# First stage of a Fourier layer: input tiles in spread pairs, batch one kept in SBUF and written by quads

## The chip, the cores and the metric

One core of one Trainium2 chip runs the whole program; the host only lays out inputs before and the output after. The metric is the device time of one execution in microseconds; several executions are timed and their median counts.

## The reference

Two batches of 3008 rows of 256 numbers go through a Fourier layer (transform along the sequence, a complex matrix per frequency, a soft threshold, the inverse transform), and the 6016 resulting rows through two feed-forward layers.

```python
X = np.fft.rfft(x, axis=1)                       # x: (2, 3008, 256)
Yr = Xr @ w_r - Xi @ w_i + b_r
Yi = Xr @ w_i + Xi @ w_r + b_i
Y  = shrink(Yr, 0.01) + 1j * shrink(Yi, 0.01)    # sign(a) * max(|a| - 0.01, 0)
y  = np.fft.irfft(Y, n=3008, axis=1)
h  = y @ w_in                                    # 256 -> 2048
y  = (h * clip(h + 3, 0, 6) / 6) @ w_out
y  = (silu(y @ w_gate) * (y @ w_val)) @ w_out2   # 256 -> 1536 -> 256
```

## The kernel before

The engines are TensorE (PE, with its weight loads PEld), VectorE (DVE), ScalarE (ACT), GpSimd (POOL) and SyncE (SP). The order of instructions is written out by hand: a list `seq` of steps that a loop runs one after the other, each appending to every engine's own queue. An engine takes its queue strictly in order and waits on semaphores. SP issues nearly all DMAs and ACT those that store what ACT and DVE evicted; an issue waits for the data that it needs, for room in the tile that it fills, and for an earlier DMA whose semaphore it shares (eight semaphores go round among the DMAs of SP and ACT). SP's and ACT's transfers each have a ring on the same 16 DMA engines.

The transform of length 3008 = 47 x 64 is split. **Stage one** (`pre`, lines 239 to 254) takes, for each batch, eight tiles of 94 rows (padded to 96) by 4 x 256 columns; a tile is two matmuls of 512 columns with the table `fwd1`, evicted by ACT (first half) and DVE (second half) to a ring tile `bs`, and written to a scratch in memory `Bd` by ACT. `load_x` reads x three tiles ahead, into two pairs of buffers. **Stage two** (`s2`, lines 281 to 294) works on a quad, four of the 24 frequency groups at a time, six quads (Q) per batch: `load_q` (lines 273 to 279) reads a table `m` and the quad's 16 of the 96 rows of `Bd`, over all columns, as `z`. So z of any quad needs all eight tiles of its batch in memory. ACT and DVE evict the result as a high and a low part, X. **The product** (`ln`, lines 305 to 326) multiplies with the complex weights `linh` and `linl`, two halves per quad with 24 matmuls each, reads a table `n`, and steps a conversion `conv1`. **The last step** (`ia`, lines 328 to 336) goes back within the quad and writes `Cd`.

`conv1` (class `Convert`, lines 137 to 189) turns the first feed-forward weights, which arrive as 64-bit words in 32 pieces `st` of 256 KB, into a high and a low part `w1h` and `w1l`: one piece per step, in stages on DVE and ACT. `Convert.load` on SP waits for a free `st` buffer of four.

`seq` (lines 366 to 378) runs stage one of batch one and three tiles of batch two, then stage two of quad 0, and then for each quad p: half a product, half a last step of quad p - 1, a tile of batch two while there are any, stage two of quad p + 1 (which issues the reads of quad p + 2), the other half of the product, another tile, another half of a last step. From quad 8 on, `unit()` mixes in the first feed-forward layer, in blocks of about 500 tokens; `load_ct` and `post` read `Cd` and finish the inverse transform of a block. The second feed-forward layer follows.

`prepare` (lines 228 to 237) issues the reads of the weights `lin`, of the bias and of the table `inv2` on POOL's queue and splits lin into `linh` and `linl` there. Ahead of everything PE runs three warm-up matmuls on zeros.

Of the kernel before, what the change touches and what calls it, by code (L numbers as in the profile page):

```python
# [40 lines left out]
def dft_tables():  # L41


    tp = 2 * np.pi
    n1 = np.arange(N1)
    f = np.zeros((N1, NG, 2))
    for g in range(NG):
        a = tp * ((n1 * g) % N1) / N1
        f[:, g, 0], f[:, g, 1] = np.cos(a), -np.sin(a) * (g > 0)
    fwd1 = np.zeros((2, N1, NG, 2, 2))  # L50
    for q in range(2):
        fwd1[q, :, :, q, :] = f
# [20 lines left out]
    out = {"fwd1": fwd1, "inv2": fwd1.T, "fwd2": fwd2, "inv1": inv1}  # L73
    return {n: np.ascontiguousarray(v, dtype=np.float32) for n, v in out.items()}
# [3 lines left out]
def fourier_moe_kernel(ctx: ExitStack, tc: tile.TileContext, x, lin, bias, w1, w2, fwd1, inv2, fwd2,  # L78
# [9 lines left out]
    Bd = [dram.tile([GW, NJ * DIM], F32, name=f"Bd{b}") for b in range(NB)]  # L88
# [32 lines left out]
    fwd1_sb = misc.tile([QP, GW], F32, name="fwd1_sb")  # L121
# [15 lines left out]
    class Convert:  # L137
# [11 lines left out]
        def load(self, i):  # L149
            t = wst.tile([128, 256], I64, tag="st", name="st", bufs=4)  # L150
            nc.sync.dma_start(t, self.pieces[i][0])
# [24 lines left out]
        def high(self, i):  # L176
            nc.scalar.copy(self.pieces[i][1], self.full[i])

        def low(self, i):
            _, hi, lo = self.pieces[i]  # L180
# [10 lines left out]
    def pieces(p, name, src, nf, n, into):  # L191
        out = []
        for f in range(nf):
            t = [p.tile([128, n, 256], F32R, name=f"{name}{i}_{f}") for i in "hl"]
            into[f] = t
            out += [(src[:, f, j], t[0][:, j], t[1][:, j]) for j in range(n)]
        return Convert(out)
# [7 lines left out]

    def ring4(name):
        return ap_.tile([128, 4 * DIM], F32, tag="bc", name=name, bufs=4)


    NT = NJ // 4  # L210
    xt = {}
# [8 lines left out]
    for n in range(3):  # L220
        load_x(n)
# [4 lines left out]
    conv1 = pieces(w1p, "w1", w1, KF1, 2, W1)  # L226

    def prepare():
# [3 lines left out]
        nc.gpsimd.dma_start(inv2_sb, inv2)  # L232
# [5 lines left out]

    def pre(n):
        b, i = divmod(n, NT)  # L240
        load_x(n + 3)
        bs = ring4(f"bs{b}_{i}")
        for h in range(2):
            p = psf[0]([GW, 512], f"p1_{b}_{i}_{h}")
            nc.tensor.matmul(p, fwd1_sb, xt[n][:QP, h * 512 : (h + 1) * 512], start=True, stop=True)
            o = bs[:GW, h * 512 : (h + 1) * 512]
            if h == 0:
                nc.scalar.copy(o, p)
            else:
                nc.vector.tensor_copy(o, p)  # L250
# [22 lines left out]
    def load_q(b, Q):  # L273
        if (b, Q) in z_t or Q >= NQ:
            return
        if Q not in m_t:
            m_t[Q] = table("m", fwd2, Q, f"m{Q}", 6)
        z_t[b, Q] = ap_.tile([128, 4, DIM], F32, tag="z", name=f"z{b}_{Q}", bufs=3)
        nc.sync.dma_start(z_t[b, Q], bview[b][:, Q * 4 : Q * 4 + 4, :])

    def s2(b, Q, dh):

        if dh == 0:
            X[b, Q] = [ap_.tile([128, 2, 4, 3 * K2], F32R, tag=f"x{k}", name=f"x{k}_{b}_{Q}", bufs=2) for k in "hl"]
# [75 lines left out]
    def pre_conv(n):  # L360
        pre(n)
        if n > NT:
# [3 lines left out]
    seq = P[:1] + [prepare] + P[1:NT] + [lambda: load_q(0, 0)] + P[NT : NT + 3] + S(0)  # L366
    rest = P[NT + 3 :]
    for p in range(len(ORDER)):
        l, a = L(p), A(p - 1)
        some, rest = rest[:2], rest[2:]  # L370
        u = [lambda: unit()] if p >= FROM else []
        seq += [l[0], a[0]] + u + some[:1] + S(p + 1)[:1] + u + S(p + 1)[1:] + [l[1]] + u + some[1:] + [a[1]] + u
        if p == NQ:
            seq += [lambda: load_ct(blocks[0])]
# [23 lines left out]
    def pair(p, tag):  # L398
        return [p.tile([128, 2, BLK], F32R, tag=f"{tag}{i}", name=f"{tag}{i}", bufs=2) for i in "hl"]
# [164 lines left out]
    conv2 = Convert2([(w2[:, f, j], None, None) for f in range(KF2) for j in range(3)])  # L564
# [244 lines left out]
```

## Time and profile before

| | us |
|---|---|
| median of 3 runs | 1247.07 |
| range of the runs | 1246.85 to 1248.23 |
| the profiled execution, its time | 1247.67 |
| the profiled execution, its span in the trace | 1245.9 |
| idle time of PE between 28.0 and 34.3 us | 6.3 |

The median is the metric. The profile is of one execution whose own time, 1247.67, is 1.77 above its span, as the time counts what lies around the first and the last instruction. In the trace, times count from the span's start. [...] The chain of waits is followed back from the last instruction; read forward, each piece is what the next one waited for. `p L245` is a matmul of stage one, `p L287` of stage two, `p L113` to `L115` of the product, `p L333` of the last step.

### The profile page before, as it was taken

To read this page: it belongs to the slowest core of one execution; us is meant where nothing else is said; L and a number is where in the kernel's file an instruction comes from. 1 tells how busy PE (TensorE), PEld (TensorE's weight loads), DVE (VectorE), ACT (ScalarE), POOL (GpSimd) and SP (SyncE) were. 2 spreads that over 40 slices of the span, in tenths; PEclk is the share of its full clock that TensorE was granted. 3 is DMA by queue.
4 is the path that set the end of the run, shared out by engine and by line. 5 is a ranking of instruction groups with operands and counts; after the bars stand their busy time and mean duration, and the time that the engine had idled before them with its cause. 6 is when DMAs were issued, how large, how long until landed. Compare 5 with 4: busy or idle time off the path is not lost.

```text
span 1245.9 us, 15942 instructions
## 1 busy us (share of the span) xinstructions
PE 1228.3 (99%) x5914; PEld 1034.2 (83%) x5914; DVE 809.8 (65%) x1424; ACT 679.7 (55%) x1216; POOL 6.3 (1%) x15
## 2 busy tenths in 40 slices
PE   7899999999999999999999999999999999999998
PEld 2799987888888888888899888888888888888997
DVE  2587665666666666666656577676676676676665
ACT  2455544555555555555555566656656555656554
POOL 2000000000000000000000000000000000000000
PEclk9899999999999999999999999999999999999999
DMA  9976323033122122132032244554644644544551
GB/s 305 279 258 191 102 77 105 28 100 103 64 91 93 59 70 93 64 100 91 39 105 91 72 175 170 203 182 152 220 158 170 235 153 152 216 157 168 203 186 72
DMA packets 50285, 172.84 MB, mean 139 GB/s; under 512 B 4752, under 2 KB 18160, under 8 KB 39456
## 3 DMA queue, kind: packets, MB, share of 16 engines
q1 hardware_dynamic: 41856, 158.55, 37.4%
q10 hardware_dynamic: 8128, 12.58, 2.8%
q8 instruction: 46, 0.75, 0.2%
q0 software_dynamic: 224, 0.69, 0.2%
q14 instruction: 31, 0.25, 0.1%
HBM read 132.75 MB, written 39.06 MB: 138 GB/s over the span
## 4 chain that ended last, share of the span: by engine, by line
PE 96%; DMA 2%; DVE 0%; ACT 0%; issue 0%; SPq 0%; ACTq 0%; DVEq 0%
PE acc L114 12%; PE acc L115 12%; PE acc L113 12%; PE ph L113 7%; PE ph L115 7%; PE ph L114 7%; PE P L662 5%; PE P L663 5%; PE P L664 5%; PE Tb L663 3%; PE Tb L662 3%; PE Tb L664 3%; PE p L419 3%; PE p L113 2%; PE p L115 2%; PE p L114 2%
## 5 line engine op out<-in xcount | busy, mean ns | idle before, releaser
L434 DVE SCALAR_TENSOR_TENSOR r<-r,ph 128x512 f32<-128x512 f32 (+1 forms) x192 | 129.7, 676 | 83.3 <-ACT r L433 82.8
L118 DVE TENSOR_TENSOR gl<-r,gh 128x512 fp32r<-128x512 f32 (+1 forms) x192 | 130.1, 678 | 82.4 <-ACT gh L452 81.0
L433 ACT ACTIVATE r<-ph,three 128x512 f32<-128x512 f32 (+1 forms) x192 | 130.2, 678 | 96.1 <-PE ph L115 80.6
L452 ACT CAST gh<-r 128x512 fp32r<-128x512 f32 (+1 forms) x192 | 117.3, 611 | 84.4 <-DVE r L434 82.7
L113 PE MATMUL ph<-xah,w1l 128*128 128x512 f32 (+1 forms) x384 | 152.1, 396 | 0.0
L113 PE MATMUL acc<-gh,w1l 128*128 128x512 f32 (+1 forms) x384 | 148.3, 386 | 1.5 <-ACT gh L452 1.5
L114 PE MATMUL acc<-gl,w1h 128*128 128x512 f32 (+1 forms) x384 | 148.2, 386 | 0.2 <-DVE gl L118 0.2
L115 PE MATMUL ph<-xah,w1h 128*128 128x512 f32 (+1 forms) x384 | 148.2, 386 | 0.0
L114 PE MATMUL ph<-xal,w1h 128*128 128x512 f32 (+1 forms) x384 | 148.1, 386 | 0.0
L115 PE MATMUL acc<-gh,w1h 128*128 128x512 f32 (+1 forms) x384 | 148.1, 386 | 0.0
L118 DVE TENSOR_TENSOR gl<-s,gh 128x512 fp32r<-128x512 f32 (+1 forms) x144 | 97.3, 676 | 49.8 <-ACT gh L686 49.7
L662 PE MATMUL P<-xo,slot 128*128 128x512 f32 (+1 forms) x288 | 111.3, 386 | 1.7 <-DVE g L732 0.8
L114 PE MATMUL acc<-gl,slot 128*128 128x512 f32 (+1 forms) x288 | 111.1, 386 | 0.3 <-DVE gl L118 0.2
L113 PE MATMUL acc<-gh,slot 128*128 128x512 f32 (+1 forms) x288 | 111.0, 385 | 0.0
L664 PE MATMUL P<-xo,slot 128*128 128x512 f32 (+1 forms) x288 | 110.9, 385 | 0.0
L115 PE MATMUL acc<-gh,slot 128*128 128x512 f32 (+1 forms) x288 | 110.9, 385 | 0.0
L663 PE MATMUL P<-xo,slot 128*128 128x512 f32 (+1 forms) x288 | 110.9, 385 | 0.0
L728 ACT ACTIVATE s<-g 128x512 f32<-128x512 f32 (+1 forms) x72 | 44.9, 623 | 93.7 <-DVE g L726 93.7
L686 ACT CAST gh<-s 128x512 fp32r<-128x512 f32 (+1 forms) x144 | 88.1, 612 | 1.5 <-DVE s L745 1.2
L113 PEld LDWEIGHTS acc<-gh,w1l 128*128 128x128 f32 x384 | 72.1, 188 | 15.4 <-ACT gh L452 1.9
L114 PEld LDWEIGHTS acc<-gl,w1h 128*128 128x128 f32 x384 | 72.1, 188 | 14.6 <-DVE gl L118 0.9
L115 PEld LDWEIGHTS ph<-xah,w1h 128*128 128x128 f32 x384 | 72.1, 188 | 14.0
(94 smaller groups left out, 2258.7 us busy)
## 6 DMA issues: line engine op xcount, KB each, us to landing
slot<-Wd SPq DMA_DIRECT2D x72, 1152.0 KB, 5.1
st<-in_w SPq DMA_DIRECT2D x68, 256.0 KB, 3.8
Wd<-slot SPq DMA_DIRECT2D x12, 1152.0 KB, 4.7
x<-in_x SPq DMA_DIRECT2D x16, 384.0 KB, 6.5
Bd<-bs ACTq DMA_DIRECT2D x16, 384.0 KB, 5.9
z<-Bd SPq DMA_DIRECT2D x12, 512.0 KB, 6.1
Cd<-cs ACTq DMA_DIRECT2D x12, 512.0 KB, 3.5
Xd<-x SPq DMA_DIRECT2D x20, 256.0 KB, 2.1
```

Source lines behind the costliest of these rows:

```text
L113: nc.tensor.matmul(o, wl, xh, start=start, stop=False)
L114: nc.tensor.matmul(o, wh, xl, start=False, stop=False)
L115: nc.tensor.matmul(o, wh, xh, start=False, stop=stop)
L118: nc.vector.tensor_tensor(out=o, in0=full, in1=hi.bitcast(F32), op=ALU.subtract)
L433: nc.scalar.activation(r[:, :n], p[:, :n], AF.Relu, bias=three)
L434: nc.vector.scalar_tensor_tensor(out=r[:, :n], in0=r[:, :n], scalar=6.0, in1=p[:, :n], op0=ALU.min, op1=ALU.mult)
L452: nc.scalar.copy(hi[:, :n], g[:, :n])
L662: nc.tensor.matmul(o, wl, x[:, 0, :n], start=start, stop=False, skip_group_check=not start)
L663: nc.tensor.matmul(o, wh, x[:, 1, :n], start=False, stop=False, skip_group_check=not start)
L664: nc.tensor.matmul(o, wh, x[:, 0, :n], start=False, stop=True, skip_group_check=not start)
L686: nc.scalar.copy(hi[:, :nb], t[:, :nb])
L728: nc.scalar.activation(s0[:, :n], h, AF.Silu)
```

## The change

**Input.** The host lays x out in pairs of tiles, 96 rows by 2048 columns (768 KB) in one contiguous piece. `load_x(k)` reads pair k. The first pair comes as two DMAs of a tile each into partitions 0 to 95 as before; every other pair as two DMAs, 64 rows into the even partitions and 32 rows into every fourth, so that the rows spread over all 128 partitions; the 32 partitions between are cleared by memsets first (pair 1 by DVE, pairs 2 and 3 by POOL). The table `fwd1` gets a second half of 128 rows for the spread form. The four pairs of batch one have four places (two borrowed from the tiles X) and are issued at once; the pairs of batch two reuse the first two places, after tiles 4, 6, 9, and the last one after quad 1.

**Batch one's stage one** is evicted to one tile `first` in SBUF (room that later holds half of w1) and written by quads: the columns of `fwd1` are reordered so that quad Q's 16 rows are partitions Q, Q + 6, and so on; each quad has its own scratch. Quad 0 is written by ACT in four parts after tiles 3, 5, 6 and 7; `group(Q + 1)` is written by SP just ahead of the read of quad Q.

**Batch two's stage one:** the first four tiles go to a tile `second` (room of the other half of w1) and are written by SP in one DMA of 1536 KB after quad 0; the others as before. Five of its tiles instead of three now stand before the loop over the quads, and one per quad, from quad 1 on, instead of two.

**The rest.** w1 lies in two large tiles, X and the blocks' inputs in one tile each for high and low part; `inv2` is read by SP after quad 6; `conv1` steps with tiles from 12 on instead of 9; writes that wait are sent at the end of each quad too.

```diff
+    both = np.zeros((128, 2 * GW))
+    mixed = fwd1.reshape(QP, NG // 4, 16).transpose(0, 2, 1).reshape(QP, GW)
+    both[:QP, :GW] = mixed
+    both[::2, GW:], both[1::4, GW:] = mixed[:64], mixed[64:]
...
-    Bd = [dram.tile([GW, NJ * DIM], F32, name=f"Bd{b}") for b in range(NB)]
+    Bd = [dram.tile([16 if n < NQ else GW, NJ * DIM], F32, name=f"Bd{n}") for n in range(NQ + 1)]
...
-    def load_x(n):
-        b, i = divmod(n, NT)
-        if b < NB:
-            xt[n] = xs_p.tile([128, 4 * DIM], F32, tag="xah" if n % 2 else "xal", name=f"x{b}_{i}", bufs=2)
-            nc.sync.dma_start(xt[n][:QP], x[b][:, i * 4 * DIM : (i + 1) * 4 * DIM])
+    def load_x(k):
+        t, src = room[k], x[k * 2 // NT, k % (NT // 2)]
+        if k == 0:
+            for n in range(2):
+                nc.sync.dma_start(t[:QP, n * TC : (n + 1) * TC], src[:, n * TC : (n + 1) * TC])
+        else:
+            nc.sync.dma_start(t[::2], src[:64])
+            nc.sync.dma_start(t[1::4], src[64:])
...
+    for k in range(4):
+        if k < 2:
+            room[k] = xs_p.tile([128, 2 * TC], F32, tag="xa", name=f"room{k}", bufs=2)
+        else:
+            room[k] = ap_.tile([128, 3 * TC], F32, tag="X", name=f"room{k}", bufs=2)[:, : 2 * TC]
+        for h in range(2 if k else 0):
+            (nc.vector if k == 1 else nc.gpsimd).memset(room[k][:, h * TC : (h + 1) * TC], 0.0)
+        load_x(k)
+    nc.gpsimd.memset(room[0][96:], 0.0)
+    for k in range(4, NB * NT // 2):
+        room[k] = room[k % 2]
...
     def pre(n):
+        sent()
         b, i = divmod(n, NT)
-        load_x(n + 3)
-        bs = ring4(f"bs{b}_{i}")
+        if b == 0:
+            o = first[:GW, i * TC : (i + 1) * TC]
+        elif i < 4:
+            o = second[:GW, i * TC : (i + 1) * TC]
+        else:
+            o = ring4(f"bs{b}_{i}")[:GW]
...
-        sent()
-        out_b.append(lambda: nc.scalar.dma_start(Bd[b][:, i * 4 * DIM : (i + 1) * 4 * DIM], bs[:GW]))
-        if i == NT - 1:
+        if n in SINCE:
+            c = slice(SINCE[n] * TC, (i + 1) * TC)
+            out_b.append(lambda: nc.scalar.dma_start(Bd[0][:, c], first[0:GW:NQ, c]))
+        elif b and i >= 4:
+            out_b.append(lambda: nc.scalar.dma_start(bd1[:, :, i * TC : (i + 1) * TC], o))
+        if n == NT - 1:
             sent()
+        if n in REFILL:
+            load_x(REFILL[n])
+
+    REFILL = {4: 4, 6: 5, 9: 6}
+    SINCE = {3: 0, 5: 4, 6: 6, 7: 7}
+    bd1 = Bd[NQ].rearrange("(q r) c -> r q c", q=NQ)
+
+    def group(Q):
+        if 0 < Q < NQ:
+            nc.sync.dma_start(Bd[Q], first[Q:GW:NQ])
+
+    def write_second():
+        nc.sync.dma_start(bd1[:, :, : 4 * TC], second[:GW, : 4 * TC])
...
+        if b == 0:
+            group(Q + 1)
...
-        if n > NT:
+        if n >= NT + 4:
             conv1.step()
...
-    seq = P[:1] + [prepare] + P[1:NT] + [lambda: load_q(0, 0)] + P[NT : NT + 3] + S(0)
-    rest = P[NT + 3 :]
+    seq = [prepare] + P[:NT] + [lambda: load_q(0, 0)] + P[NT : NT + 2] + [lambda: load_q(0, 1)]
+    seq += P[NT + 2 : NT + 4] + S(0) + P[NT + 4 : NT + 5]
+    rest = P[NT + 5 :]
...
-        some, rest = rest[:2], rest[2:]
+        some = [rest.pop(0)] if p and rest else []
...
+        seq += [sent]
+        if p < 2:
+            seq += [lambda: load_x(7)] if p else [write_second]
```

Where instructions stand now, at three places. First SP's queue from the last reads of x ahead of quad 0 on (`x1_2` is batch two's tile 2, `z0_0` quad 0 of batch one, `Bd0` a scratch, `room0` and `room1` the places of x). Before:

```order
L217 DMA x1_1_221<-in_x 96x1024
L217 DMA x1_2_231<-in_x 96x1024
L270 DMA m0_242<-in_fwd2 128x512
L279 DMA z0_0_244<-Bd0_60 128x4x256
L217 DMA x1_3_246<-in_x 96x1024
L217 DMA x1_4_255<-in_x 96x1024
L151 DMA st_265<-in_w1 128x256
L217 DMA x1_5_267<-in_x 96x1024
L151 DMA st_277<-in_w1 128x256
L270 DMA m1_279<-in_fwd2 128x512
```

And in the changed kernel:

```order
L226 DMA room1_116<-in_x 64x2048
L227 DMA room1_116<-in_x 32x2048
L296 DMA Bd1_61<-first_136 16x8192
L315 DMA m0_206<-in_fwd2 128x512
L327 DMA z0_0_208<-Bd0_60 128x4x256
L226 DMA room0_113<-in_x 64x2048
L227 DMA room0_113<-in_x 32x2048
L296 DMA Bd2_62<-first_136 16x8192
L315 DMA m1_225<-in_fwd2 128x512
L327 DMA z0_1_227<-Bd1_61 128x4x256
```

The read of quad 0 now has one write of a group and its table ahead of it, and behind it a pair of x, the next group and the next quad, where single tiles of x and pieces `st` of w1 stood.

Second, SP's queue around the last read of x (`x1_7` before, the second `room1` pair in the changed kernel) and quad 3 (`z0_3`). Before:

```order
L270 DMA m2_357<-in_fwd2 128x512
L279 DMA z0_2_359<-Bd0_60 128x4x256
L151 DMA st_387<-in_w1 128x256
L217 DMA x1_7_420<-in_x 96x1024
L151 DMA st_437<-in_w1 128x256
L270 DMA n1_439<-in_inv1 128x512
L151 DMA st_449<-in_w1 128x256
L151 DMA st_503<-in_w1 128x256
L270 DMA m3_505<-in_fwd2 128x512
L279 DMA z0_3_507<-Bd0_60 128x4x256
```

And in the changed kernel (`second` and `first` are the kept tiles, `n1` the last step's table):

```order
L299 DMA Bd6_66<-second_137 16x6x4096
L315 DMA n1_365<-in_inv1 128x512
L155 DMA st_372<-in_w1 128x256
L155 DMA st_423<-in_w1 128x256
L296 DMA Bd4_64<-first_136 16x8192
L315 DMA m3_426<-in_fwd2 128x512
L327 DMA z0_3_428<-Bd3_63 128x4x256
L155 DMA st_457<-in_w1 128x256
L226 DMA room1_116<-in_x 64x2048
L227 DMA room1_116<-in_x 32x2048
```

The last read of x stood ahead of quad 3's read and right behind quad 2's; now it stands behind quad 3's read, behind the write of 1536 KB and behind a group's write.

Third, PE's queue around stage two of quad 0 (`p1_1_2_0` is stage one, batch two, tile 2, first half; `p2_0_0_0` stage two of quad 0, first half). Before:

```order
L245 MATMUL p1_1_0_0_249<-x1_0_211,fwd1_sb_82 96x512
L245 MATMUL p1_1_0_1_252<-x1_0_211,fwd1_sb_82 96x512
L245 MATMUL p1_1_1_0_258<-x1_1_221,fwd1_sb_82 96x512
L245 MATMUL p1_1_1_1_261<-x1_1_221,fwd1_sb_82 96x512
L245 MATMUL p1_1_2_0_270<-x1_2_231,fwd1_sb_82 96x512
L245 MATMUL p1_1_2_1_273<-x1_2_231,fwd1_sb_82 96x512
L287 MATMUL p2_0_0_0_285<-m0_242,z0_0_244 128x128 x4
L287 MATMUL p2_0_0_1_294<-m0_242,z0_0_244 128x128 x4
```

And in the changed kernel:

```order
L275 MATMUL p1_1_2_0_229<-room1_116,fwd1_sb_87 96x512
L275 MATMUL p1_1_2_1_232<-room1_116,fwd1_sb_87 96x512
L275 MATMUL p1_1_3_0_235<-room1_116,fwd1_sb_87 96x512
L275 MATMUL p1_1_3_1_238<-room1_116,fwd1_sb_87 96x512
L336 MATMUL p2_0_0_0_242<-m0_206,z0_0_208 128x128 x4
L336 MATMUL p2_0_0_1_251<-m0_206,z0_0_208 128x128 x4
L275 MATMUL p1_1_4_0_261<-room0_113,fwd1_sb_87 96x512
L275 MATMUL p1_1_4_1_264<-room0_113,fwd1_sb_87 96x512
```

Tile 3 of batch two has moved ahead of stage two, and tile 4 stands between it and the first product (the rows after these are the product's in both).

## Rows read from the trace of the kernel before

**Rows 1.** Page of the whole run: span; busy time by engine; the last chain by engine.

```profile
span 1245.9 us, 15942 instructions
PE 1228.3 (99%) x5914; PEld 1034.2 (83%) x5914; DVE 809.8 (65%) x1424; ACT 679.7 (55%) x1216; POOL 6.3 (1%) x15
...
PE 96%; DMA 2%; DVE 0%; ACT 0%; issue 0%; SPq 0%; ACTq 0%; DVEq 0%
```

**Rows 2.** Windows of PE: stretch, length, busy (instructions), granted clock, DMA share, GB/s.

```profile
6.12:21.50 15.38, 14.51 (x33) 1.00 1.03 330
21.50:28.00 6.50, 5.67 (x12) 1.00 1.03 376
28.00:34.30 6.30, 0.00 (x0) 0.88 0.94 283
34.30:39.75 5.45, 5.35 (x22) 0.51 1.04 248
39.75:42.50 2.75, 2.42 (x20) 1.00 1.08 401
42.50:60.00 17.50, 17.50 (x116) 1.00 0.92 279
```

**Rows 3.** Waits of PE over the whole run: us in total, times, longest.

```profile
PE p L287 <- DMA z<-Bd: 6.4, 1, 6.4
PE p L245 <- DMA x<-in_x: 1.6, 3, 0.7
```

**Rows 4.** Chain of waits, 0 to 75 us: start us, us, what.

```profile
21.54 0.70 DVE bs L250
22.30 6.03 DMA Bd<-bs
28.45 5.74 DMA z<-Bd
34.33 2.06 PE p L287 x8
...
42.56 1.72 PE p L245 x4
44.28 1.79 PE p L287 x16
...
48.94 1.72 PE p L245 x4
...
53.54 0.86 PE p L333 x4
```

**Rows 5.** DMA issues from 20 to 30 us: count, KB each, median us to landing.

```profile
Bd<-bs ACTq DMA_DIRECT2D x4, 384.0 KB, 4.9
...
z<-Bd SPq DMA_DIRECT2D x1, 512.0 KB, 5.7
```

**Rows 6.** DMA issues from 134 to 142 us, where the rings are otherwise nearly empty.

```profile
z<-Bd SPq DMA_DIRECT2D x1, 512.0 KB, 3.7
```

**Rows 7.** DMA issues of the whole run: a short write to memory.

```profile
Xd<-x SPq DMA_DIRECT2D x20, 256.0 KB, 2.1
```

**Rows 8.** Windows of all engines; the last three columns: granted clock, DMA share, GB/s.

```profile
10.00:28.00 18.00, 17.00 (x38) 5.45 (x36) 6.18 (x9) 5.45 (x10) 2.71 (x5) 1.00 1.02 358
28.50:49.50 21.00, 14.77 (x86) 12.83 (x87) 6.80 (x14) 6.47 (x16) 0.00 (x0) 0.84 1.02 300
30.00:40.00 10.00, 5.35 (x22) 4.85 (x22) 1.38 (x2) 2.08 (x6) 0.00 (x0) 0.66 1.00 263
```

**Rows 9.** Timeline, 0 to 35 us: start us, us, engine, line, operation.

```profile
0.94 0.48 DVE L127 MEMSET zeros<- 128x512 f32 x1
...
6.12 1.88 PE L245 MATMUL p<-x,fwd_sb 96*96 96x512 f32 x4
...
8.24 0.40 POOL L236 CAST linh<-lin_st 128x256 fp32r<-128x256 f32 x1 [5.25 <-DMA lin_st<-in_lin]
```

More of the change, by code (lines that the diff above doesn't have):

```diff
@@ L120, in fourier_moe_kernel @@
     misc = pool(ctx, "misc", "left")
-    fwd1_sb = misc.tile([QP, GW], F32, name="fwd1_sb")
+    fwd1_sb = misc.tile([128, 2 * GW], F32, name="fwd1_sb")
     inv2_sb = misc.tile([GW, QP], F32, name="inv2_sb")
@@ L176, in high @@
         def high(self, i):
-            nc.scalar.copy(self.pieces[i][1], self.full[i])
+            f, j = divmod(i, 2)
+            nc.scalar.copy(weights(f)[0][:, j], self.full[i])
         def low(self, i):
-            _, hi, lo = self.pieces[i]
+            f, j = divmod(i, 2)
+            hi, lo = (t[:, j] for t in weights(f))
             nc.vector.tensor_tensor(out=lo, in0=self.full.pop(i), in1=hi.bitcast(F32), op=ALU.subtract)
@@ L189, in step, with weights @@
                     stage(at)
[L191 to L197, printed above, removed]
+    HALF = KF1 // 2
+    def weights(f):
+        if f not in W1:
+            t = w1p.tile([128, HALF, 2, 2, 256], F32R, tag=f"w1_{f // HALF}", name=f"w1_{f // HALF}", bufs=1)
+            for i in range(HALF):
+                W1[f - f % HALF + i] = [t[:, i, k] for k in range(2)]
+        return W1[f]
     xs_p = pool(ctx, "rings", "left")
@@ L225, in fourier_moe_kernel @@
         nc.tensor.matmul(p, zeros[:, :128], zeros, start=True, stop=True)
-    conv1 = pieces(w1p, "w1", w1, KF1, 2, W1)
+    conv1 = Convert([w1[:, f, j] for f in range(KF1) for j in range(2)])
     def prepare():
@@ L231, in prepare @@
         nc.gpsimd.dma_start(bias_sb, bias)
-        nc.gpsimd.dma_start(inv2_sb, inv2)
         for dh in range(2):
@@ L237, in prepare @@
                 nc.gpsimd.tensor_tensor(out=lo, in0=st, in1=hi.bitcast(F32), op=ALU.subtract)
+    first = w1p.tile([128, NT * TC], F32, tag="w1_1", name="first", bufs=1)
+    second = w1p.tile([128, NT * TC], F32, tag="w1_0", name="second", bufs=1)
     def pre(n):
+        sent()
         b, i = divmod(n, NT)
-        load_x(n + 3)
-        bs = ring4(f"bs{b}_{i}")
+        if b == 0:
[4 more added lines that the diff above has]
+            o = ring4(f"bs{b}_{i}")[:GW]
         for h in range(2):
             p = psf[0]([GW, 512], f"p1_{b}_{i}_{h}")
-            nc.tensor.matmul(p, fwd1_sb, xt[n][:QP, h * 512 : (h + 1) * 512], start=True, stop=True)
-            o = bs[:GW, h * 512 : (h + 1) * 512]
+            rhs = room[n // 2][:, (2 * (n % 2) + h) * 512 : (2 * (n % 2) + h + 1) * 512]
+            if n < 2:
+                nc.tensor.matmul(p, fwd1_sb[:QP, :GW], rhs[:QP], start=True, stop=True)
+            else:
+                nc.tensor.matmul(p, fwd1_sb[:, GW:], rhs, start=True, stop=True)
             if h == 0:
-                nc.scalar.copy(o, p)
+                nc.scalar.copy(o[:, :512], p)
             else:
-                nc.vector.tensor_copy(o, p)
-        sent()
-        out_b.append(lambda: nc.scalar.dma_start(Bd[b][:, i * 4 * DIM : (i + 1) * 4 * DIM], bs[:GW]))
-        if i == NT - 1:
-            sent()
+                nc.vector.tensor_copy(o[:, 512:], p)
+        if n in SINCE:
[4 more added lines that the diff above has]
+        if n == NT - 1:
+            sent()
+        if n in REFILL:
[8 more added lines that the diff above has]
+        nc.sync.dma_start(bd1[:, :, : 4 * TC], second[:GW, : 4 * TC])
     out_b = []
@@ L278, in load_q @@
         z_t[b, Q] = ap_.tile([128, 4, DIM], F32, tag="z", name=f"z{b}_{Q}", bufs=3)
-        nc.sync.dma_start(z_t[b, Q], bview[b][:, Q * 4 : Q * 4 + 4, :])
+        src = bview[NQ][:, Q * 4 : Q * 4 + 4, :] if b else bview[Q]
+        nc.sync.dma_start(z_t[b, Q], src)
     def s2(b, Q, dh):
         if dh == 0:
-            X[b, Q] = [ap_.tile([128, 2, 4, 3 * K2], F32R, tag=f"x{k}", name=f"x{k}_{b}_{Q}", bufs=2) for k in "hl"]
+            t = ap_.tile([128, 2, 2, 4, 3 * K2], F32R, tag="X", name=f"X{b}_{Q}", bufs=2)
+            X[b, Q] = [t[:, k] for k in range(2)]
         p = psf[0]([128, 4, 128], f"p2_{b}_{Q}_{dh}")
@@ L398, in pair @@
     def pair(p, tag):
-        return [p.tile([128, 2, BLK], F32R, tag=f"{tag}{i}", name=f"{tag}{i}", bufs=2) for i in "hl"]
+        t = p.tile([128, 2, 2, BLK], F32R, tag=tag, name=tag, bufs=2)
+        return [t[:, k] for k in range(2)]
     def load_ct(k):
@@ L562, in steps @@
                 yield
-    conv2 = Convert2([(w2[:, f, j], None, None) for f in range(KF2) for j in range(3)])
+    conv2 = Convert2([w2[:, f, j] for f in range(KF2) for j in range(3)])
     steps = conv2.steps()
```

15 lines of the change are left out of this document (7 added, 8 removed).

## Prediction

> **What bounds the kernel now.** I read the page first, then PE's windows, PE's waits, the chain of waits, and last the DMA issues with their landing times. TensorE (PE) is busy 99% of the span and the chain that ended last runs 96% through PE [rows 1], so only three things can move the end: PE work removed, PE idle time removed, or time at the lower clock removed. The change removes no matmul. [...] The chain says what z waits for: the last eviction of batch one's stage one at 21.54, its write to memory, 6.03 us, the read of the first quad, 5.74 us, and then stage two starts at 34.33 [rows 4]. Both transfers are slow because the rings are full: DMA share is about 1.0 from 10 to 49.5 us, at 358 and then 300 GB/s [rows 8]; the same read takes 3.7 us when little else moves [rows 6]. So the head is bounded by bytes in flight, and by stage two needing the whole of batch one written.
>
> **The change part by part.** Times are on the trace's axis. A stage-one tile costs PE 1.72, a quad's stage two 1.79, a half of the product 44.28 + 1.79 to 48.94, or 2.87, a half of the last step 0.86 [rows 4].
>
> First, **stage one of batch one**. It starts at 6.12, when the warm-up matmuls end [rows 9]; nothing in the change touches that. Its evictions stay in SBUF, so the 3.1 MB of writes leave the rings, and x comes as pairs. Eight tiles end at 6.12 + 8 x 1.72 = 19.9, if x keeps up. The memsets that clear the unused rows stand ahead of the second to fourth pair: on DVE 0.48 us per 512 columns [rows 9], so 2.0 for pair two; on POOL 0.40 per 256 columns [rows 9], at most 1.6 per 1024 if a memset runs like that cast, and 3.2 for each of pairs three and four. Pair four is then issued near 7, while it is needed at 6.12 + 6 x 1.72 = 16.4: hidden by the pairs ahead of it. POOL's load of lin moves behind them (some 10 us); its operands are first used after 30. I charge 0.5 us for x arriving late (0 to 1.6, all of PE's waits for x now [rows 3]).
>
> Second, **quad 0's way through memory**. Only its last 64 KB wait for tile 7: eviction 0.70 [rows 4], to 20.6. The write lands 2.1 us later if it is like the short write on free rings [rows 7], 4.9 if like the tile writes on full ones [rows 5]; I take 3.5, since only one group write stands beside it: 24.1. SP waits for this at z's issue, with the rest of its queue behind. The read takes 3.7 [rows 6] to 5.7 [rows 5]; the middle, 4.7, gives 28.8 for the start of stage two (bounds 26.8, where PE's twelve tiles end, and 31.2), against 34.33. PE idles 2.0 us instead of 6.3, so I assume the clock stays up.
>
> Third, **the order of PE**. Twelve tiles instead of eleven stand ahead of stage two, and a thirteenth between it and the first product. That tile covers evictions: now both halves need from 36.41 to 40.09, 3.7 us [rows 4], in which PE partly waits. After: 28.8 + 1.79 + 1.72 + 2.87, plus 0.5 for what the tile does not cover, is 35.7. The row before that answers to it is the tile at 42.56 [rows 4], with 11 tiles done; two more are worth 3.44. Gain so far: 42.56 + 3.44 - 35.7 = **10.3 us**.
>
> Fourth, **what is late next**. The bytes are postponed, not removed. From z0's issue at 24.1 SP queues in this order: z0, pair 7 of 8, group 2, m1, z1, st, n0, st, group 3, m2, z2, st, the 1536 KB write of batch two's four kept tiles, n1, st, st, group 4, m3, z3, st and the last pair of x: 9,472 KB. ACT adds two tiles and one quad of results, 1,280 KB. Together 11.0 MB before batch two's tile 6 can run. PE reaches that tile after the product half at 35.7, then two stage twos, four product halves, three last-step halves and one tile: 3.58 + 11.48 + 2.58 + 1.72 = 19.4, at 55.1. Full rings moved 358 GB/s where rows were long and much was written, 300 where the small tables were read [rows 8]; the new mix has both, so 330: 33.3 us. A landing adds 1.4 (2.1 less 256 KB at 358 [rows 7, 8]). The pair lands at 24.1 + 33.3 + 1.4 = 58.8, so PE waits **3.7 us** there; at 300 it waits 7.0, at 371 not at all. Everything queued on PE behind that tile waits, SP does not. The other reads have more slack: z3 stands before this pair, z4 is due 13 us after it. As this wait sets the end, an earlier or later z0 moves the end only by z0's issue, some 1.4 us to either side.
>
> Fifth, **edits that I cost at nothing**. The 128-row matmuls have the columns of the 96-row ones. W1 in two large tiles, hi and lo in one: the same instructions on the same engines. The conversion of w1 runs three steps later and catches up beside the units of block one; DVE's free 35% [rows 1] hides it. The first high part now waits for the 1536 KB write; that lands near 24.1 + 21.0 + 1.4 = 46.5 (6.9 MB at 330), when ACT has the evictions of quad 2, some 50, still ahead of it; if it is late, ACT holds the evictions behind it and PE loses what it is late by. The inverse table (36 KB) moves to SP after quad 6: far from its use.
>
> Sum: 10.3 - 3.7 - 0.5 = 6.1 us off the profiled execution's 1247.67, which is 0.60 above the median; against the median 1247.07, **1241.0**.
>
> [...]
>
> **The rivals.** *No second wait.* If long rows lift the rings to 371 GB/s, the last pair is in time: 10.3 - 0.5 = 9.8, **1237.3**. For it: 376 GB/s from 21.5 to 28 [rows 2]. Against: tables and quads are half of the bytes, and moved at 300. Chance 0.20.
>
> *Sixteen-row writes cost double.* Three groups stand in the queue before the last pair; 512 KB at 330 is 1.6 us, so 4.8 more: the wait becomes 8.5. PE's clock fell during an idle time of 6.3 us [rows 2], so it would fall here too; 5.35 us of work at half speed cost 2.7 [rows 2]. Together 10.3 - 0.5 - 8.5 - 2.7 = -1.4, **1248.5**. [...] Chance 0.15.
>
> *Slower: the rings stay at their worst.* From 30 to 40 us full rings moved only 263 GB/s [rows 8], under reads of x, st and the tables. At that rate 11.0 MB take 41.8, the pair lands at 67.3, PE waits 12.2 and pays 2.7 for the clock: 10.3 - 0.5 - 14.9 = -5.1, **1252.2**. It decides below 280 GB/s, where wait and clock exceed the gain by 2.5 us. Against it: half of the bytes are now in rows of 4 KB or more. Chance 0.10.
>
> *The early write is not early.* If the last 64 KB are held behind group 1's 32 KB rows until z0 is issued at 28.4 as now [rows 4], all that follows shifts by 4.3: 6.1 - 4.3 = 1.8, **1245.3**. Chance 0.05.
>
> **How the numbers follow.** The forecast, a closed head and a second wait of 1 to 6 us, has 0.50: 1241.0. About 0.2% (2.5 us) is what a measurement of this kernel tells from no change. Faster: nearly all of the forecast, rival one and a little of rival two, 0.70. Slower: rival three and a fifth of rival two, 0.13. The rest, 0.17, within. The range leaves out rival three, the upper part of rival two and the outer part of rival one (a start of stage two at 26.8 without a second wait would be 1235): 1236.0 to 1248.5.
>
> **What would show it.** Right: stage two's first matmul at 27 to 31 with a clock of 1.00; PE's wait for z below 3 us; a wait of PE for x, on the first-stage line, near 55 us, of 1 to 6 us; after that PE full as before. DMA share near 1.0 from 24 to 59. Wrong, if PE never waits near 55 (rival one), if the group writes take over 6 us to land (rival two), if the rings move below 290 GB/s from 24 to 59 (rival three), or if ACT's first high part of w1 waits for microseconds on a DMA.

## The result, and the profile after

The changed kernel takes **1256.88 us** (median of four runs, 1254.54 to 1258.60); the kernel before takes 1247.01 beside it. The ratio is 1.0076, with a 95% interval of 1.0058 to 1.0093: slower by some 9.9 us. Forecast were 1241.0 us with a range of 1236.0 to 1248.5; the time lies above the range. The profiled execution took 1258.60 us.

The page of the changed kernel, in the lines of [rows 1], and one of its groups of layer one, the first feed-forward layer (line, operation, count; busy us, mean ns of one):

```profile
span 1256.8 us, 15921 instructions
PE 1240.8 (99%) x5914; PEld 1033.7 (82%) x5914; DVE 811.7 (65%) x1426; ACT 679.9 (54%) x1216; POOL 11.1 (1%) x19
...
L119 PE MATMUL acc<-gh,w 128*128 128x512 f32 (+1 forms) x384 | 149.7, 390 | 0.0
```

The same group of the page of before:

```profile
L115 PE MATMUL acc<-gh,w1h 128*128 128x512 f32 (+1 forms) x384 | 148.1, 386 | 0.0
```

The head went nearly as forecast. The chain of waits from 17 to 66 us, to be laid beside [rows 4]:

```profile
20.25 0.70 DVE first L279
21.01 1.89 DMA Bd<-first
22.97 5.09 DMA z<-Bd
28.07 0.14 issue
28.20 1.14 PE p L336 x8
...
36.34 1.79 PE p L336 x16
...
52.91 7.33 DMA room<-in_x
60.24 0.14 issue
60.38 3.62 PE p L275 x4
64.00 1.78 PE p L336 x16
```

Stage two starts at 28.20 and not at 34.33, and the second wait, for the last pair of x, ends at 60.24. PE's windows (stretch, length, busy and instructions, granted clock as a share of full speed, mean busy share of the 16 DMA engines, GB/s) and its longest wait:

```profile
35.00:50.00 15.00, 15.00 (x117) 1.00 0.81 310
50.00:60.00 10.00, 5.72 (x42) 1.00 0.89 291
60.00:70.00 10.00, 9.62 (x54) 0.83 0.84 277
```

```profile
PE p L275 <- DMA room<-in_x: 4.7, 1, 4.7
```

When the first block's input of the feed-forward part is made, the changed kernel is still 3.1 us ahead, as the timelines show (start, length, operation; before first, then after):

```profile
120.51 2.77 PE L419 MATMUL p<-inv_sb,ct 96*128 96x94 f32 x24
```

```profile
117.41 2.77 PE L473 MATMUL p<-inv_sb,ct 96*128 96x94 f32 x24
```

From there on PE is full in both kernels, at a granted clock of 1.00, with the same matmuls. It gets through fewer of them. Windows of PE, before first, then after (the number in brackets is the matmuls that started):

```profile
300.00:350.00 50.00, 50.00 (x236) 1.00 0.22 70
825.00:875.00 50.00, 50.00 (x222) 1.00 0.42 150
925.00:975.00 50.00, 50.00 (x222) 1.00 0.47 166
```

```profile
300.00:350.00 50.00, 50.00 (x231) 1.00 0.22 69
825.00:875.00 50.00, 50.00 (x217) 1.00 0.42 149
925.00:975.00 50.00, 50.00 (x223) 1.00 0.46 165
```

All of layer one is 2% slower (300 to 350 stands for it; from 400 to 600 us 916 matmuls start, and 936 before), and so are stretches of layer two, the second feed-forward layer: of its six pairs of blocks, those that take their combined inputs xo from a right-side pool (825 to 875); the pairs between them (925 to 975) are as before. No wait and no clock differs there, and the rings move about the same (69 GB/s against 70, 149 against 150). So three questions were put to the chip: what slows the matmuls, what sets the second wait, and what spreading x is worth.

### The profile page after: what moved, and what is told of

It is laid out like the page before. It is cut to its first block, busy times and chain, and to the rows that moved or that the text cites. A ratio compares the mean times of both kernels' runs of the same rounds, so it can differ in the third digit from the quotient of the medians.

```text
span 1256.8 us, 15921 instructions
## 1 busy us (share of the span) xinstructions
PE 1240.8 (99%) x5914; PEld 1033.7 (82%) x5914; DVE 811.7 (65%) x1426; ACT 679.9 (54%) x1216; POOL 11.1 (1%) x19
## 4 chain that ended last, share of the span: by engine, by line
PE 97%; DMA 2%; DVE 1%; ACT 1%; issue 0%; SPq 0%; ACTq 0%; DVEq 0%
PE acc L118 12%; PE acc L119 12%; PE acc L117 12%; PE ph L117 7%; PE ph L119 7%; PE ph L118 7%; PE P L716 5%; PE P L718 5%; PE P L717 5%; PE Tb L718 3%; PE Tb L717 3%; PE Tb L716 3%; PE p L473 3%; PE p L117 2%; PE p L119 2%; PE p L118 2%
## 5 line engine op out<-in xcount | busy, mean ns | idle before, releaser
L117 PE MATMUL ph<-xa,w 128*128 128x512 f32 (+1 forms) x384 | 153.4, 400 | 0.0
L117 PE MATMUL acc<-gh,w 128*128 128x512 f32 (+1 forms) x384 | 149.8, 390 | 1.0 <-ACT gh L506 1.0
L118 PE MATMUL acc<-gl,w 128*128 128x512 f32 (+1 forms) x384 | 149.9, 390 | 0.3 <-DVE gl L122 0.2
L119 PE MATMUL ph<-xa,w 128*128 128x512 f32 (+1 forms) x384 | 149.8, 390 | 0.0
L118 PE MATMUL ph<-xa,w 128*128 128x512 f32 (+1 forms) x384 | 149.7, 390 | 0.0
L119 PE MATMUL acc<-gh,w 128*128 128x512 f32 (+1 forms) x384 | 149.7, 390 | 0.0
L117 PEld LDWEIGHTS acc<-gh,w 128*128 128x128 f32 x384 | 72.3, 188 | 16.6 <-ACT gh L506 1.4
L118 PEld LDWEIGHTS acc<-gl,w 128*128 128x128 f32 x384 | 72.3, 188 | 16.1 <-DVE gl L122 1.0
L119 PEld LDWEIGHTS acc<-gh,w 128*128 128x128 f32 x384 | 72.3, 188 | 15.1
```

Source lines behind the costliest of these rows:

```text
L117: nc.tensor.matmul(o, wl, xh, start=start, stop=False)
L118: nc.tensor.matmul(o, wh, xl, start=False, stop=False)
L119: nc.tensor.matmul(o, wh, xh, start=False, stop=stop)
```

## What slows the matmuls

What differs between the two programs in those stretches is where tiles stand in SBUF. The stage-one table grew from 96 to 192 columns, from 384 to 768 bytes per partition. It is the first tile on the left side, so everything placed above it there (xa, r, gh, gl and layer two's slot, xo and T) moved up by 384 bytes. The weights of layer one and xo of layer two's odd pairs stand on the right side and did not move. That all of these start at one offset modulo 512 in the kernel before is worked out from the sizes of its tiles, not read from a trace. The names: xa is the input that the first matmuls of layer one (ph) read, gh and gl are the high and low part that the accumulations (acc) read, r is a work tile of ACT and DVE, slot holds layer two's weights. The **theory**: the offset between tiles that PE reads together costs time. The **rival**: something else in the change does (the idle time at 55 us, the large tiles, other transfers).

**E1, the changed kernel with 512 bytes of shift and not 384.**

```
-    fwd1_sb = misc.tile([128, 2 * GW], F32, name="fwd1_sb")
+    fwd1_sb = misc.tile([128, 2 * GW + 32], F32, name="fwd1_sb")[:, : 2 * GW]
```

> The changed kernel with the table of stage one made 128 bytes wider per partition (unused), so that all that lies above it on the left side of SBUF moves by 512 bytes against the kernel before and not by 384. No instruction changes. Theory one (the shift by 384 bytes is what makes the 512-column matmuls slower): 1244, the 3 us that the changed kernel is ahead when stage one ends, with PE busy near 1228 and the layer-one accumulations at 386 ns. Theory two (the matmuls are slower for something else in the change: the idle time at 55 us, the large tiles, the transfers): 1257, PE busy 1240, accumulations at 390 ns.

**E2, the kernel before with the shift alone.**

```
-    fwd1_sb = misc.tile([QP, GW], F32, name="fwd1_sb")
+    fwd1_sb = misc.tile([QP, GW + 96], F32, name="fwd1_sb")[:, :GW]
```

> The kernel before with its stage-one table 384 unused bytes wider per partition: the addresses on the left side are those of the changed kernel, all else is before. Theory one (the shift): slower, 1259 to 1260, PE busy near 1240, layer-one accumulations at 390 ns. Theory two (something else in the change): 1247, no change.

**E3, the changed kernel with the right side moved too.**

```
-EDGE = 480
+EDGE = 608
```

> The changed kernel with the unused strip at the top of the right side made 128 bytes longer, so that weights and other right-side tiles move down by 128 bytes: left and right then stand at the same offset to each other modulo 512 as before, though both are 384 off a multiple of 512. Theory one in the form that the offset between the two operands of a matmul counts: 1244. Theory one in the form that an operand off a multiple of 512 counts: 1257 or more, up to 1260, since layer two's tiles of the right side are now off too. Theory two: 1257.

**E4, E6 and E8, the kernel before with 256, 128 and 64 bytes of shift** (as E2, with GW + 64, GW + 32 and GW + 16).

> The kernel before with the stage-one table 256 unused bytes wider per partition. If any shift off a multiple of 512 costs the same: 1259. If the cost goes by the size of the shift or by which part of a 512-byte stretch is touched, something between 1247 and 1259 or above. Theory two: 1247.

> The kernel before with the stage-one table 128 unused bytes wider per partition. If the offset counts modulo 256 (384 was slow, 256 and 512 were not): 1261, as with 384, with layer-one accumulations at 390 ns. If 384 is slow in itself, or the cost grows with the offset: 1247 to 1252.

> The kernel before with the stage-one table 64 unused bytes wider per partition. If any offset that is no multiple of 256 costs the same: 1261. If the cost goes by the offset's size within 256: between 1247 and 1261, the layer-one accumulations between 386 and 390 ns. If only multiples of 128 that are odd cost: 1247.

What was measured (shift against the kernel before; matmuls started in two windows of 50 us, PE's busy time, from the profiles; medians and ratios from the timed runs, each ratio against runs of the kernel before on the same chip: 1247.55 beside E1 to E4, 1247.18 beside E6 and E8, 1247.01 beside the changed kernel):

| kernel | left against right, bytes | 300:350 | 825:875 | PE busy | median us | ratio, 95% |
|---|---|---|---|---|---|---|
| before | 0 | 236 | 222 | 1228.3 | 1247.55 | 1 |
| E4 | 256 | 236 | 223 | 1228.4 | 1247.06 | 0.9995 [0.9985, 1.0004] |
| E8 | 64 | 235 | 217 | 1236.8 | 1254.97 | 1.0060 [1.0046, 1.0075] |
| E6 | 128 | 231 | 217 | 1242.9 | 1261.61 | 1.0112 [1.0099, 1.0125] |
| E2 | 384 | 231 | 216 | 1243.4 | 1261.24 | 1.0115 [1.0097, 1.0134] |
| changed | 384 | 231 | 217 | 1240.8 | 1256.88 | 1.0076 [1.0058, 1.0093] |
| E1 | 512 | 236 | 223 | 1225.6 | 1244.92 | 0.9975 [0.9961, 0.9989] |
| E3 | 384 + 128 = 512 | 236 | 222 | 1227.5 | 1242.95 | 0.9965 [0.9953, 0.9977] |

The page of E1 is that of its fastest execution, 1240.59 us; its ten lie between that and 1247.51. E2, in the lines shown above for before and after:

```profile
PE 1243.4 (99%) x5914; PEld 1035.7 (82%) x5914; DVE 810.5 (64%) x1424; ACT 680.3 (54%) x1216; POOL 6.3 (0%) x15
...
L115 PE MATMUL acc<-gh,w1h 128*128 128x512 f32 (+1 forms) x384 | 149.7, 390 | 0.0
```

The rival is out: 384 unused bytes make the kernel before slower by 13.7 us, with none of the change in it, and 128 more unused bytes bring the changed kernel below the one before. E3 says that it is the offset between the sides and not the address: there the left side still stands 384 off a multiple of 512, and all is fast. Shifts of 256 and 512 cost nothing, 128 and 384 the same, 64 about half in all: layer two's odd pairs lose as much as at 128 (217), layer one less (235 matmuls from 300 to 350 us, against 236 in before and 231 in E6).

**E7, E13 and E14, which tiles.** E7 puts 128 unused bytes on the left just ahead of gh, in the kernel before, so gh, gl and layer two's left tiles move and xa does not. E13 is E6 with the same strip, so that of the tiles that the feed-forward layers' products read only xa is off; r, ct and the tiles of the conversion move with it. E14 is E2 with 128 unused bytes above the right-side xo.

```
         ct[k] = xs_p.tile([GW, NP, DIM], F32, tag="ct", name=f"ct{k[0]}", bufs=1)
+        if k == blocks[0]:
+            xs_p.tile([128, 32], F32, name="strip")
```

```
             nc.scalar.copy(B[p][m][:, 0, :n], x())
+            if p == 1 and 'strip' not in T:
+                T['strip'] = p2.tile([128, 32], F32, name="strip")
```

> The kernel before with an unused strip of 128 bytes put between the ring of the inverse step's inputs and the ring gh, so that only gh, gl and layer two's left-side tiles move; xa (the moving operand of the first matmuls of layer one) stays. If the pair of operands of each matmul counts: in layer one only the accumulations (gh, gl against w) are slower, 390 against 386 ns, the first matmuls (ph) stay at 386; total 1252 to 1255. If one shifted operand slows every matmul that runs near it, since a weight load runs beside the matmul before it: both are slower, 1259 to 1261. If gh is not what counts: 1247 to 1250.

> The kernel before with the stage-one table 128 bytes wider and a second unused strip of 128 bytes ahead of gh: xa, r and ct on the left are moved by 128 bytes, gh, gl and layer two's left tiles by 256, which is harmless. Theory (each operand that a matmul streams counts by its offset to the weights next to it, modulo 256): layer one is slower through xa alone, ph 389 to 390 ns and the accumulations between 386 and 389; layer two is as before, 222 matmuls in 50 us in all its stretches; the cost is what the shift of all (14.4) leaves beside the shift of gh, gl and layer two (9.9): 4.5, so 1251 to 1253. Rival (only gh, gl or layer two's tiles count): 1247 to 1248.

> The kernel before with the left side moved by 384 bytes, as in the second experiment, and with an unused strip of 128 bytes that moves the right-side tiles of layer two's odd pairs by 128, so that in these pairs xo stands at the same offset as slot and gh again. Theory (the offset between operands counts, not the address): layer one as slow as with the shift (231 matmuls from 300 to 350 us), layer two's odd pairs as fast as before (222 in 825 to 875, where the shift gave 216), 1254 to 1258 in all. Rival (an address off a multiple of 256 counts by itself, or layer two's odd pairs are slow for another reason): 1260 to 1262, 216 or 217 matmuls there.

| kernel | off the common offset | 300:350 | 825:875 | median us | ratio, 95% |
|---|---|---|---|---|---|
| E7 | gh, gl, layer two's left tiles | 233 | 216 | 1257.05 | 1.0079 [1.0066, 1.0092] |
| E13 | xa (with r, ct) | 233 | 222 | 1253.60 | 1.0047 [1.0032, 1.0062] |
| E14 | left side against w1 only | 230 | 223 | 1256.68 | 1.0070 [1.0054, 1.0087] |

Layer two's odd pairs in E2 and then in E14 (windows from 825 to 875 us, groups by line and shape: busy us, mean ns):

```profile
L114 PE MATMUL acc<-gl,slot 128*128 128x512 f32 x27 | 10.7, 396 | 0.0
L115 PE MATMUL acc<-gh,slot 128*128 128x512 f32 x27 | 10.7, 395 | 0.0
L664 PE MATMUL P<-xo,slot 128*128 128x512 f32 x26 | 10.3, 394 | 0.0
```

```profile
L114 PE MATMUL acc<-gl,slot 128*128 128x512 f32 x28 | 10.9, 389 | 0.0
L115 PE MATMUL acc<-gh,slot 128*128 128x512 f32 x28 | 10.9, 389 | 0.0
L664 PE MATMUL P<-xo,slot 128*128 128x512 f32 x27 | 10.5, 389 | 0.0
```

E14 gives these pairs their speed back by moving one of the three tiles, xo, to the offset of the others. Its layer one stays slow. E2's rows also show that the price isn't paid by the odd matmul alone: acc reads gh and slot, which stand at one offset, and is as slow as P, which reads xo and slot, at two. E7's expectation that only the accumulations of layer one would be slower, at 390 against 386, was too neat in the same way: in its page one of the three is at 390 and two at 388 and 389, the first matmuls are slower too, by 1 ns, and its 1257.05 lies between the 1252 to 1255 of this theory and the 1259 to 1261 of the other. In E13, of what the products read, xa alone is off; from 300 to 500 us its first matmuls take 393 to 398 ns and the accumulations 391 or 392, against 389 in before (394 for the first of the group). So a matmul is slower also when the one beside it is off. Whether it is two reads of PE that count or a read of PE and an access of ACT or DVE, whose tiles move too, no run here settles: that placement costs the time is shown, the mechanism stays open. E7 and E13 cost 9.9 and 6.0 us, 15.9 together, near the 14.4 of E6, which moves all of these.

## What sets the second wait

In the changed kernel SP, not the rings, was late from 45 to 50 us: the rings were nearly dry, and SP was waiting (window of PE with DMA share and GB/s; then SP's waits from 36 to 54 us):

```profile
45.00:50.00 5.00, 5.00 (x37) 1.00 0.34 129
```

```profile
SPq L155 <- DVE wt L169: 6.0, 1, 6.0
SPq L296 <- DMA Bd<-bs: 4.9, 1, 4.9
```

The first row is a load of the conversion that waits for a free buffer `st`, with the rest of SP's queue behind it. SP has this wait in the kernel before too (its waits from 0 to 140 us), but there the last read of x, issued at 46.23, stands ahead of all but 4.0 us of it:

```profile
SPq L151 <- DVE wt L165: 72.2, 21, 8.5
```

The second row is a group write of SP that waits for a write by ACT with which it has nothing to do. The trace shows why: in the changed kernel the 287 transfers of SP and ACT raise eight completion semaphores, 35 or 36 each, in rotation over both engines, and none was issued before the one ahead of it on its semaphore, the eighth ahead, had landed. ACT's write issued at 40.99 and the group write issued at 48.85 raise the same semaphore, and the first landed 7.8 us after its issue, just ahead of the second. ACT issues its writes behind evictions, and the two up to 60 us landed 7.8 and 9.7 us later; whatever SP has eight places behind one waits for it, and all behind that. Both rows stand ahead of the last pair; how much of its lateness is due to each, no run separates, since E5 puts the pair ahead of both.

**E5, the last pair of x ahead of the 1536 KB write** (on E1, whose pad it keeps, as all that follow).

```
-        if p < 2:
-            seq += [lambda: load_x(7)] if p else [write_second]
+        if p == 0:
+            seq += [lambda: load_x(7), write_second]
```

> The changed kernel with the 128-byte pad of the first experiment, and one line moved: the last pair of x is loaded one quad earlier, ahead of the 1536 KB write of batch two's kept tiles. Theory one (the shift apart, what keeps the gain from 10 us is the second wait, PE waiting for the last pair of x, and it is set by where SP comes to issue that load): no wait of PE for x near 57, clock at 1.00 from 50 to 70, and 1240 to 1241, 4 us below the 1244.9 with the pad alone. Rival (it is set by the bytes in the rings, so something else queued there is late instead, z1 or z2 of batch one): PE waits as long for another tile, 1244 to 1245.

Measured 1240.50 (1238.69 to 1245.86; ratio 0.9954 [0.9936, 0.9972]). The median is the theory's, though E1's interval, [0.9961, 0.9989], overlaps with this one; two of the six executions lie at 1245. The profiled one, at 1245.46, is one of them, and there another tile is late, as the rival said: PE no longer waits for the last pair, and then waits 5.3 us for a quad, which SP issued late, at 63.22, and which took 10.7 us to land. PE's wait, SP's from 20 to 66 us, and the piece of the chain:

```profile
PE p L336 <- DMA z<-Bd: 6.8, 2, 5.3
```

```profile
SPq L155 <- DMA Bd<-bs: 10.2, 1, 10.2
SPq L296 <- DMA Cd<-cs: 6.5, 1, 6.5
```

```profile
63.22 10.74 DMA z<-Bd
```

**E9, the quads queued two ahead** (on E5).

```
             ahead(p + 1)
+            if p + 2 < NQ:
+                ahead(p + 2)
```

> The kernel with the pad and the early last pair of x, with one more line: the reads of batch one's quads (and the tables and group writes that go with them) are queued on SP two quads ahead of their use and not one. Theory one (SP's queue is held by the eight transfers that the program allows in flight, each waiting for the eighth before it, and whatever is needed first behind such a hold is late): with 11 us more room no read of a quad is late, PE waits only for z0 and for the pair of tile 4, and all executions lie at 1238 to 1240, where those at 1245 disappear. Rival (the bytes in the rings set it): the longer queue ahead of the last pair of x makes that late again, by some 2 us, 1241 to 1243.

Measured 1242.34 (1238.71 to 1248.15; 0.9965 [0.9946, 0.9984]): a miss. In the profiled execution (1241.81) the quads were in time, but st, the raw pieces of w1, was late instead: ACT, which scales them, waited for st from 50 to 70 us with the evictions of stage two behind it in its order. The rotation is still part of it: SP waited 8.6 us for a write by ACT, which was issued at 40.72 and took 10.1 us, before it could issue st at 50.81; the piece issued at 54.00 then took 8.1 us to land.

```profile
ACT head L160 <- DMA st<-in_w: 6.5, 2, 4.4
```

**E11, batch two's writes and the results' writes issued by POOL** (on E5); **E12, the same on E9.** In the changed kernel the two transfers of POOL raise two semaphores that none of SP or ACT raises. The writes also leave SP's and ACT's queues and rings for POOL's, so the edit changes more than the rotation.

```
-            out_b.append(lambda: nc.scalar.dma_start(bd1[:, :, i * TC : (i + 1) * TC], o))
+            out_b.append(lambda: nc.gpsimd.dma_start(bd1[:, :, i * TC : (i + 1) * TC], o))
...
-        nc.sync.dma_start(bd1[:, :, : 4 * TC], second[:GW, : 4 * TC])
+        nc.gpsimd.dma_start(bd1[:, :, : 4 * TC], second[:GW, : 4 * TC])
...
-            nc.scalar.dma_start(cview[b][:, Q * 4 : Q * 4 + 4, :], cs[b, Q])
+            nc.gpsimd.dma_start(cview[b][:, Q * 4 : Q * 4 + 4, :], cs[b, Q])
```

> The kernel with the pad and the early last pair of x, with the writes of batch two's stage one (kept tiles and single tiles) and of the last step's results issued by POOL and not by SP and ACT. These then take no turn in the rotation of eight completion semaphores that the transfers of SP and ACT share, so SP's next transfer no longer waits for a write that ACT issued late. Bytes and order of work on PE are the same. Theory one (SP's queue is held by that rotation): SP's waits for Bd<-bs and Cd<-cs (10.2 and 6.5 us in the kernel it stands on) are gone, no read of a quad is late, and all executions lie at 1238 to 1240. Rival (the bytes in the rings set it): SP's waits move to other names, PE still waits 2 to 5 us for a quad or an eviction between 55 and 75 us, and executions spread up to 1245 as before.

> The same edit on the kernel that queues the quads two ahead. Theory one: as with the edit alone, 1238 to 1240, and no more than 1 us apart from it. Rival: the longer queue of reads costs 2 us or more also here, since the bytes ahead of the last pair of x and of st are what it adds: 1241 to 1243.

E11 takes **1238.17** (1237.72 to 1240.61; 0.9930 [0.9916, 0.9944]), 9.4 us below the kernel before and the lowest median here. SP's largest wait is now for the conversion's own tiles (19.9 us on DVE, seven times), none is for a write of batch two or of results, the rings are full, and PE is too (windows of PE, as above):

```profile
35.00:50.00 15.00, 15.00 (x116) 1.00 1.04 405
50.00:60.00 10.00, 10.00 (x70) 1.00 0.97 339
60.00:70.00 10.00, 10.00 (x70) 1.00 0.87 281
```

E12 takes 1243.12 (0.9968 [0.9956, 0.9981]): here the rival was right. With the quads two ahead st is late whoever writes: SP no longer waits for a write by ACT, but one piece took 16.5 us from its issue at 36.50 to its landing, over rings that moved 360 GB/s from 35 to 50 us. ACT waits 6.8 us for one, PE for the evictions behind that.

```profile
ACT head L160 <- DMA st<-in_w: 8.0, 2, 6.8
```

```profile
PE p L117 <- DVE X L122: 3.7, 2, 3.0
```

So both play a part. The rotation held SP in the kernels without E11's edit (4.9 us in the changed kernel, 10.2 in E5, 8.6 in E9) and no longer with it; with that gone, the bytes decide what may be pulled ahead (E12). That the rotation alone makes the time change from one execution to the next is likely but not shown: E11's five executions lie within 2.9 us where E5's six lie within 7.2, the intervals of the two overlap, and its edit moves transfers to another ring as well.

## What spreading x is worth

**E10, x on 96 adjacent partitions again** (on E9, to be compared with it): one transfer for a pair, no cleared rows, 96-row matmuls.

```
-            nc.sync.dma_start(t[::2], src[:64])
-            nc.sync.dma_start(t[1::4], src[64:])
+            nc.sync.dma_start(t[:QP], src)
...
-        for h in range(2 if k else 0):
-            (nc.vector if k == 1 else nc.gpsimd).memset(room[k][:, h * TC : (h + 1) * TC], 0.0)
...
-    nc.gpsimd.memset(room[0][96:], 0.0)
...
-            if n < 2:
-                nc.tensor.matmul(p, fwd1_sb[:QP, :GW], rhs[:QP], start=True, stop=True)
-            else:
-                nc.tensor.matmul(p, fwd1_sb[:, GW:], rhs, start=True, stop=True)
+            nc.tensor.matmul(p, fwd1_sb[:QP, :GW], rhs[:QP], start=True, stop=True)
```

> The same kernel with x on 96 adjacent partitions, one transfer for a pair and not two, no cleared rows and 96-row matmuls in all of stage one: the spreading of the input tiles undone alone. [...] If stage one's matmuls set the pace there and the pairs are in time either way: the same time within 1 us, or up to 1 us less, since seven transfers fewer stand in the queue.

Measured 1250.46 (1.0030 [1.0017, 1.0043]), 8.1 us above E9, twice the 4 us that the author took as the most that spreading x could be worth: the pairs are not in time either way. PE's waits and its window from 5 to 28 us in E10, then the window in E9:

```profile
PE p L268 <- DMA room<-in_x: 3.5, 3, 1.5
```

```profile
5.00:28.00 23.00, 20.63 (x43) 0.93 0.97 251
```

```profile
5.00:28.00 23.00, 21.67 (x51) 1.00 0.82 293
```

With adjacent rows the rings are busier (0.97) and move less (251 GB/s); spread, they move 293 at 0.82. The kernel before, also with 96 adjacent rows, moved 330 GB/s from 6.12 to 21.50 [rows 2], reads of x and writes together; 251 is what the reads reached with few writes beside them. A pair takes 10.8 us from issue to landing, against 6.2 and 6.3 for the two parts of a spread one in the changed kernel. PE waits in stage one, its clock is at 0.93 there, stage two starts at 33.31 and not 27.90, and that is where most of the 8.1 us is (E10, then E9):

```profile
33.31 2.02 PE L329 MATMUL p<-m,z 128*128 128x128 f32 x16 [1.46 <-DMA z<-Bd]
```

```profile
27.90 2.02 PE L336 MATMUL p<-m,z 128*128 128x128 f32 x16 [1.26 <-DMA z<-Bd]
```

Without the spread stage two starts only 1.0 us earlier than in the kernel before, so most of what the head gains hangs on it. E10 also reads each later pair with one transfer and not two; no run separates that from the spread. Why the rings moved 293 GB/s with x spread and 251 without, none shows.

The second rival took the sixteen-row writes to cost double. The five group writes of SP from 5 to 66 us of the changed kernel landed 4.4 to 7.1 us after issue, 4.8 in the median; the 96-row writes of 384 KB took 4.9 in [rows 5]. The two that took 7.1 were issued at 25.55 and 30.99 among reads, and quads of the same size took 6.3 in the median:

```profile
Bd<-first SPq DMA_DIRECT2D x5, 512.0 KB, 4.8
z<-Bd SPq DMA_DIRECT2D x5, 512.0 KB, 6.3
```

So no run shows sixteen rows to be slow, and none has the rows as its only difference.

## Why the prediction was wrong, step by step

**First, stage one: right.** PE never waited for x there, and the last eviction began at 20.25, where 19.9 was worked out. POOL's memsets took 0.95 us each, less than the 1.6 at most.

**Second, quad 0's way: right.** The write took 1.89 us (3.5 taken, 2.1 the lower bound), the read 5.09 (4.7); stage two began at 28.20 (28.8), with the clock at 1.00.

**Third, the order of PE: right but for 0.6 us.** The first product half ended at 36.34 and not 35.7: PE waited 1.3 us for an eviction ahead of the tile in between. The gain is 42.56 + 3.44 - 36.34 = 9.7, where 10.3 was forecast.

**Fourth, what is late next: place and size right, cause wrong, price incomplete.** The last pair landed at 60.24 (58.8), and PE waited 4.7 us (3.7). But the step let SP issue without a pause and the rings set the time at 330 GB/s with a DMA share near 1.0; in truth the rings moved 302 GB/s from 24 to 59 us at a share of 0.85, and 129 for a while, since SP was held 6.0 us by the conversion's buffers on DVE and 4.9 by a write of ACT. That the landing came within 1.4 us of the forecast is partly luck. The step did not charge the clock, which the second and third rival did for their longer waits: it fell after 4.7 us as well (0.83 from 60 to 70), and the tile behind it took 3.62 us and not 1.72. Together 9.7 - 4.7 - 1.9 = 3.1, which is the lead at 117 us, where 6.1 was forecast.

**Fifth, edits costed at nothing: the step that failed.** "The same instructions on the same engines" was taken to mean the same durations. The step counted instructions and left out where their operands stand, and the table that grew by 384 bytes isn't named in it at all. Its price is 13.7 us by E2, in the kernel before; taking it out of the changed kernel gives back 12.0 (E1) and 13.9 us (E3). 13.7 less 3.1 is 10.6 us slower, against 10.9 by the two profiled executions and 9.9 by the medians. The other edits in this step show no wait of PE of their own: ten tiles of 128 rows took 17.33 us, 1.73 each, and ACT waits for no DMA from 20 to 75 us, so its first high part was in time.

Without the shift the change gives 1242.95 (E3) or 1244.92 (E1), inside the range, 2 to 4 us above the forecast. Rival one, no second wait, gave 1237.3, and E11, which has none, measured 1238.17, though with other edits than that rival meant. Rival two is not borne out: two of the five group writes took 7.1 us, over the 6 that it named, but the wait was 4.7 and not 8.5, and the rings were nearly dry shortly ahead of it. Rival three is out as it was put: the rings moved 302 GB/s from 24 to 59 us, above its 290, and could move 405 from 35 to 50 (E11). The early write was early (1.89 us). No rival was the case that decided; the range had room only for causes in the first 70 us.

## What to carry to other kernels

When a change alters the size of any tile, compare the addresses of the tiles that the hot matmuls read, before and after, and keep their offsets to each other at a multiple of 256 bytes (256 and 512 were free here, 64, 128 and 384 were not); a few unused bytes are the cheapest edit there is. Where queues of two engines share completion semaphores in a rotation, count the places: here a transfer waited for the eighth ahead of it, whoever issued that one (SP for a write by ACT, 4.9 us in the changed kernel and 10.2 in E5). A stage that waits for a transfer is worth less than its wait if the next transfer in the same queue has no slack: find it, and why it is issued when it is.

## What the hardware showed that was not expected

PE's rate on the 512-column matmuls here depends on where the tiles that PE reads stand to each other in SBUF, at a granted clock of 1.00 and without any idle time in the records: 236 matmuls in 50 us at shifts of 0, 256 and 512 bytes, 231 at 128 and 384, 235 at 64 (217 against 222 in layer two). The means of the page hide it, 390 against 386 ns; the count of matmuls in a window that PE fills shows it. And with x on 96 adjacent partitions the rings moved 251 GB/s at a share of 0.97 from 5 to 28 us (E10), where with x spread over 128 they moved 293 at 0.82 (E9).
